# 64-bit weights read by a leaky rectifier on ScalarE that sets sign and exponent, no sign step on VectorE, and a new order of the work

## The chip, the core and the metric

The kernel runs on one core of a Trainium2 chip. The metric is the device time of one execution in microseconds (us), the median of three runs. The engines are called by the names of the profile: PE is TensorE (PEld its weight loads), DVE is VectorE, ACT is ScalarE, POOL is GpSimd, and SP issues the DMAs.

## The reference

Attention over a narrow window and over pooled blocks, and then a gated feed-forward network on its output, cut to what matters:

```python
# q, k, v: float32, B, H, S, D = 4, 8, 768, 64
k_sum = k.reshape(B, H, 24, 32, D).max(axis=3)
v_sum = v.reshape(B, H, 24, 32, D).mean(axis=3)
scores_l = where(abs(i - j) < 16, q @ k.T / 8, -1e9)
scores_s = q @ k_sum.T / 8 + log(32)
a = softmax(concat([scores_l, scores_s]))
attn = a @ concat([v, v_sum])                      # float32
x = attn.transpose(0, 2, 1, 3).reshape(3072, 512)
# w_gate, w_val: 512 x 1536, w_out: 1536 x 512, all float64
g = x @ w_gate
out = (g / (1 + exp(-g)) * (x @ w_val) @ w_out).astype(float32)
```

The three weight matrices come in 64 bits and go to the kernel as pairs of 32-bit words. The kernel makes a 32-bit float of each pair on the chip.

## The kernel before

**The products.** PE works on fp32r operands, which hold fewer bits than fp32. Every operand of the feed-forward products is therefore split into a high and a low part (`xh` and `xl` of attention's output, `hh` and `hl` of the hidden layer, two halves of one tile `w` or `o` for weights), and every product is made three times: high by high, high by low, low by high. Batch 0 goes through plain products: `g(j,h)` and `v(j,h)` for the twelve blocks j of 128 hidden columns and two halves h, and `D(0,...)` for the output. Batches 1 to 3 make seven products in the place of eight, with sums of weight blocks (`sumA..`), which are kept in DRAM (`sf`, `ss`, `wa`) and loaded again.

**Attention.** It goes in units (k,u), half a batch k and a pair of heads u, eight by four: scores (`SC`), `max`, `scl`, six `exp`, `eps`, `rcp` and `nrm` for the softmax, transposes of the probabilities (`PP0`, `PP1`, copied from PSUM by `pt0`, `pt1`), and the output (`XO`). `values` steps copy values and pooled values to the tiles `vw` and `vn`. Attention of the next batch runs between the feed-forward products of this one.

**The decode.** A weight block is decoded in five steps of 1024 columns, and there are 18 blocks (w0 to w11, and six of o). `abs` (L991, on ACT) writes the magnitude of the upper word, read as a 32-bit float, to the tile `m`. `clamp` (L995, DVE) holds it between two bounds. `shift` (L1001, DVE) moves its bits 3 to the left and masks them, by which eight bits of the 64-bit exponent come to the place of a 32-bit float's exponent. `sign` (L1008, DVE) takes the top bits of the raw word and sets them. `low` (L1014, DVE) adds three bits of the lower word. Then `hi` (ACT, the copy helper L513) rounds to fp32r, and `lo` (the subtraction helper L518, DVE or POOL) makes the rest. These blocks are decoded in the first 190 us, beside attention of batches 0 and 1 and the plain products of batch 0.

**The order.** Each step names the engines that may run it, its estimated cost, and the buffers that it reads and writes. `order()` is a list planner: at each turn the free engine takes the waiting step with the earliest due time. A table `NUDGES` shifts due times of single steps, gives a slack to some PE steps, and names the engine for some. `moved_behind()` then takes a hand-written table `MOVES` of 103 pairs: the first step of a pair is put right behind the second in its engine's row. The result is the order in which each engine issues its work. `WARM` names three PE steps ahead of which filler products run (5 ahead of SC(0,1), 6 ahead of XO(0,0), 1 ahead of PP1(0,2)).

Of the kernel before, what the change touches and what calls it, by code (L numbers as in the profile page):

```python
# [213 lines left out]
kt(0,1) -104.1; q(0,1) -74.3; vn(1) -74.9; kt(0,3) -72.8; q(0,2) +4.6; bias_sb +93.2; eps(0,1) -93.8 p; SC(0,3) s0.2  # L214
fv(3) -24.8 d; PP0(0,1) s0.6; pt0(0,1) +183.2 a; pt1(0,1) -26.3; FV(0) s4.6; fv(0) +54.5 d; nrm(0,2) +49 p
PP1(0,3) s0.6; XO(0,1) s1.3432; xh(1,0) +2.1 d; val2(3) +44.5 p; XO(0,3) s1.8; xh(3,0) +0.9 d; pt1(0,0) +44.3
raw_w0 -2.8; abs_w0 +68.8; lo_w0 -39.8; wa0 +27.3; odd1(0) +180.1; val2(0) -123.8 p; odd1(2) +53 a; val1(2) +4.8 p
val2(2) +1.3 p; abs_w1 +117.3; clamp_w1 +327.1; sign_w1 -90.9; q(1,0) +61.9; SC(1,0) s3.3; scl(1,0) -76.7 d
mul(0,0) -222.6; hh(0,0,0) -10.3 d; hl(0,0,0) +67.7 d; raw_w2 +31.8; sumA22_w2 +113.7 d; sumA12_w2 -32.4 d
scl(1,1) -72.2; exp0(1,1) +31.1; pt1(1,0) -84.2 d; values(1,1) +306.9; pt0(1,1) -39.1 d; pt1(1,1) -100.1  # L220
exp5(1,3) -130.7; eps(1,3) -102.1 p; raw_o0 +33.8; clamp_o0 +68.2; shift_o0 +158.4; low_o0 +72.2; raw_o2 +66.9
hi_o2 +67.7; raw_w3 -24.5; shift_w3 -150.5; sign_w3 +11.1; sumA11_w3 +76.8 d; values(1,2) +103.5 d; PP0(1,2) s1.9
PP1(1,2) s1.1; pt1(1,2) +145.2 d; values(1,3) +10.9 a; hl(0,1,1) -22.1 p; hh(0,2,1) -9.5 a; hh(0,3,1) -144.4 d
hl(0,3,1) +196.9 d; sf4 +110.8; hl(0,4,0) +78 d; kt(1,0) +154.6; pool(1,0) +198.5; vpool(1,0) +112.7; kw(2,1) +169.5
join(2,1) -183.7 a; exp4(2,0) +66; exp4(2,1) +59.7; eps(2,1) +55.4 p; lo_w5 +24.3 d; sumA22_w5 -122.2 p
silu(5,0) +105.9; hl(0,5,0) -46.5 p; PP0(2,0) s0.4; pt0(2,1) +21.4 d; values(2,1) +11.4 p; mul(5,1) +121.6
part(0,1,1) +60.9; part(0,1,2) +100.7; join(2,2) -267.6 p; join(2,3) -100.3 p; nrm(2,2) +43.9 d; SC(2,3) s1.5
nrm(2,3) -78.4 p; part(0,1,4) +34.9; abs_w6 +76.2; lo_w6 +123 p; hl(0,6,0) +84.9 d; pt0(2,3) +58.9 d; pt1(2,3) +63.6
# [5 lines left out]
shift_w9 +106.6; low_w9 -47; lo_w9 +182.3 p; wa9 -114.8; mul(9,1) -94.8; hh(0,9,1) +1.7 d; PP0(3,2) s5.3
values(3,3) +72.6 p; shift_w10 +191.5; lo_w10 +161.1 p; abs_o10 +60.5; clamp_o10 +204.2; shift_o10 +307.3
sumA22_w0 -33.5 p; sumA11_w0 -63.1 d; hi_w11 +92.3; sumA21_w1 -12.5 d; T3(1,0) +1.3 p; B11l(1,0) -69.3 p
B11h(1,1) -344.8; T3h(1,1) -126.8 d; T3l(1,1) +73.6 p; T4(1,1) -66.4 p; B22l(1,1) +42.9 p; q(4,0) -85.6
pool(2,0) +200.3; vpool(2,0) +53.6; exp2(4,0) +57.8; eps(4,0) -48.7 p; nrm(4,0) -2.8 p; ttr0(4,1) +110.7
exp1(4,1) +28.6; exp3(4,1) +86.5; eps(4,1) +82.4 p; s1(1,1) -125.4 d; hl(1,1,0) +90.2 p; mul(1,1,1) +79.4 d
hh(1,1,1) +97.8; ls(1,2) -73.1; c21(1,2) +190.8; pool(2,2) +155.6; vpool(2,2) +79.6; join(4,2) -39.6 p  # L240
join(4,3) +57.8 a; exp5(4,2) -52.6; exp0(4,3) +41.9; silu(1,3,0) +123.2; mul(1,4,1) +214.2; values(4,2) -142.4 p
join(5,0) +141.8 a; join(5,1) +167.7 a; eps(5,0) -13.1 p; SC(5,1) s5; ttr0(5,1) +131.9; eps(5,1) -4 p
nrm(5,1) -316.8 p; sumA22_w6 -24.1 p; s7(1,6) -21.7 a; hh(1,6,0) -272.9 d; hl(1,6,0) -15.2 p; mul(1,6,1) +1.6 p
PP0(5,0) s7.7; PP1(5,0) s2.8; values(5,1) -20.6 p; la(1,7) +104.2; ls(1,7) +86; sh(7) +115.8 a; sl(7) -19.1 p
ss(7) +117.1; mul(1,7,0) -26.2 p; hh(1,7,1) +55.6 d; sumA21_w8 -2.4 d; q(5,2) -28.4; XO(5,1) s4.6; exp4(5,2) +60.5
ttr0(5,3) -67.1; part(1,2,2) +80.9; sumA22_w9 +18.6 p; sumA12_w9 +55.6 p; sl(9) +14.2 p; values(5,3) +42.1 p
sumA12_w10 +28.4 p; sl(10) -26.9 p; sumA21_w11 +157 p; T3l(2,0) -80.7 d; T2l(2,0) +16.6 d; T1(2,1) +39.9 p
B11h(2,1) +120.8 d; join(6,1) -81.7 p; exp2(6,0) +67.3; exp3(6,0) +68; s1(2,1) -6.7 d; hh(2,1,1) +112.3 a
hh(2,2,1) -100.6 d; pt0(6,0) +0.6 a; pt1(6,0) +65.7 d; pool(3,2) +188.8; join(6,2) +56.6 a; join(6,3) +195.4 a
exp3(6,2) -70.8; exp4(6,2) -113; exp5(6,2) -27.7; eps(6,2) +37.4 p; exp1(6,3) -100.6; exp2(6,3) -28.7  # L250
exp5(6,3) +145; eps(6,3) +11.7 p; c22(2,3) -14.1 p; kw(7,0) -55.9; kw(7,1) -75.1; hl(2,8,1) +24.2 p
join(7,3) -10.1 p; vv(2,11) -98.1; u2(2,11) -100
# [41 lines left out]
)  # L294


def moved_behind(out):

    lists = {}
    for i, s in enumerate(out):  # L300
        s.rank = i
        lists.setdefault(s.engine, []).append(s)
    named = {s.name.replace(" ", "_"): s for s in out}
    for pair in MOVES.split("; "):
        x, y = (named[n] for n in pair.split())
        line = lists[x.engine]
        line.remove(x)
        line.insert(line.index(y) + 1, x)
    marks = set(lists.pop(None, []))
    done, again = set(), []  # L310
    while marks or any(lists.values()):
        heads = [l[0] for l in lists.values() if l] + list(marks)
        s = min((h for h in heads if all(o in done for o in h.after)), key=lambda h: h.rank)
        if s.engine is None:
            marks.remove(s)
        else:
            lists[s.engine].pop(0)
# [1259 lines left out]
```

## Time and profile before

| | us |
|---|---|
| median of three runs | 675.69 |
| the three runs | 677.05, 675.03, 675.69 |
| span of the profiled execution | 675.2 |
| PE busy | 661.9 (98%) |
| PE's weight loads busy | 609.4 (90%) |
| DVE busy | 502.0 (74%) |
| ACT busy | 374.1 (55%) |
| POOL busy | 129.8 (19%) |

The profile shows no other time of that execution than its span, which is 0.45 us under the median at two decimals (675.24). The granted clock of PE is at its upper level, 2.4 GHz, in all of the span. The page gives busy times over the whole span. The timeline of one engine says of every instruction how long the engine stood idle before it and which event ended that, and a table of windows gives busy times by stage.

### The profile page before, as it was taken

Reading aid. Unit: us, or ns where it says so; the run is one execution under the profiler, and the core shown is the slowest. Engines: PE = TensorE matmul, PEld = TensorE weight load, DVE = VectorE, ACT = ScalarE, POOL = GpSimd, SP = SyncE. Lnnn points to the kernel's source line nnn. Section 1 sums busy time; section 2 is a strip of 40 time slices with the busy share of each in tenths; the row PEclk is TensorE's granted clock in tenths of the full one; section 3 lists DMA queues with packets and bytes.
Section 4 is the critical chain, followed back from the end, with each engine's and each line's share of the span. In section 5 each row is a group of like instructions: output and inputs, shape, how many; then the busy total and the mean of one; then the engine's idle time right before and its main releaser. Section 6 shows DMA issues by size and latency. Waiting matters only on the chain.

```text
span 675.2 us, 13289 instructions
## 1 busy us (share of the span) xinstructions
PE 661.9 (98%) x5059; PEld 609.4 (90%) x5059; DVE 502.0 (74%) x1073; ACT 374.1 (55%) x901; POOL 129.8 (19%) x141
## 2 busy tenths in 40 slices
...
GB/s 343 387 296 289 310 227 332 263 248 337 310 238 160 247 312 217 318 274 218 241 205 250 160 295 154 225 215 111 252 67 201 155 253 76 230 97 222 106 109 95
DMA packets 39681, 152.71 MB, mean 226 GB/s; under 512 B 4352, under 2 KB 8896, under 8 KB 32704
## 3 DMA queue, kind: packets, MB, share of 16 engines
q1 hardware_dynamic: 39616, 151.85, 63.1%
...
## 4 chain that ended last, share of the span: by engine, by line
PE 74%; DVE 10%; DMA 3%; ACT 3%; issue 3%; POOL 0%; DVEq 0%; POOLq 0%; ACTq 0%
PE p L1197 36%; PE acc L1269 26%; PE xo L812 3%; PE g L1155 2%; PE pp L779 2%; DMA s<-ss 2%; PE v L1155 2%; PE sc L660 2%; DVE m_w L1008 1%; DMA s<-sf 1%; DVE m_w L1014 1%; DVE m_w L995 1%; DVE a L518 1%; DVE part L518 1%; ACT L1131 1%
## 5 line engine op out<-in xcount | busy, mean ns | idle before, releaser
L1269 PE MATMUL acc<-o,hh 128*128 128x512 f32 x570 | 177.8, 393 | 1.3 <-DVE a L518 1.3
L1269 PEld LDWEIGHTS acc<-o,hh 128*128 128x128 f32 x570 | 105.4, 188 | 23.9 <-DVE a L518 1.8
L1197 PE MATMUL p<-xh_T,s 128*128 128x384 f32 x432 | 122.7, 339 | 0.3 <-DMA s<-ss 0.2
L1269 PE MATMUL acc<-o,hl 128*128 128x512 f32 x285 | 111.4, 391 | 0.0
L1197 PE MATMUL p<-xh_B,wa 128*128 128x384 f32 x288 | 84.9, 335 | 0.0
L1197 PEld LDWEIGHTS p<-xh_T,s 128*128 128x128 f32 x432 | 79.0, 188 | 2.8 <-DMA s<-ss 1.3
L513 ACT CAST hh<-a 128x384 fp32r<-128x384 f32 x73 | 37.5, 513 | 71.9 <-DVE a L518 69.2
L1197 PE MATMUL p<-xl_T,s 128*128 128x384 f32 x216 | 72.3, 335 | 0.0
L513 ACT COPY s<-p 128x384 f32<-128x384 f32 x64 | 30.6, 478 | 73.4 <-PE p L1197 73.0
L518 DVE TENSOR_TENSOR part<-acc,part 128x512 f32<-128x512 f32 x71 | 47.4, 684 | 26.2 <-PE acc L1269 26.0
L1269 PEld LDWEIGHTS acc<-o,hl 128*128 128x128 f32 x285 | 53.5, 188 | 11.8 <-DVE hl L518 0.3
L518 DVE TENSOR_TENSOR hl<-a,hh 128x384 fp32r<-128x384 f32 x84 | 50.1, 597 | 14.9 <-ACT hh L513 12.1
L703 ACT ACTIVATE p<-p,nm 128x120 f32<-128x120 f32 x144 | 55.2, 385 | 4.4 <-DVE nm L691 4.0
L518 DVE TENSOR_TENSOR c<-p,u 128x384 f32<-128x384 f32 x72 | 39.6, 551 | 21.4 <-PE p L1197 21.3
L1155 PE MATMUL g<-xh_B,w 128*128 128x384 f32 x192 | 53.8, 339 | 1.7 <-ACT a L1131 1.3
L1155 PE MATMUL v<-xh_B,w 128*128 128x384 f32 x192 | 53.6, 338 | 0.0
L1197 PEld LDWEIGHTS p<-xh_B,wa 128*128 128x128 f32 x288 | 53.1, 188 | 0.1
L1197 PE MATMUL p<-xl_B,wa 128*128 128x384 f32 x144 | 48.2, 334 | 0.0
L1197 PE MATMUL p<-xh_B,s 128*128 128x384 f32 x144 | 42.6, 336 | 1.1 <-DVE v L518 1.1
L518 DVE TENSOR_TENSOR a<-c,a 128x384 f32<-128x384 f32 x65 | 36.9, 568 | 7.4 <-ACT a L1131 4.1
L1197 PE MATMUL p<-xh_T,wa 128*128 128x384 f32 x144 | 42.3, 334 | 0.0
L691 DVE CUSTOM_DVE_ANT_0 p<-sc,bias_sb 128x120 f32<-128x120 f32 x144 | 30.5, 276 | 14.4 <-PE sc L660 14.1
(161 smaller groups left out, 1360.6 us busy)
## 6 DMA issues: line engine op xcount, KB each, us to landing
...
```

Source lines behind the costliest of these rows:

```text
L513: nc.scalar.copy(out, in_)
L518: vector[e].tensor_tensor(out=out, in0=a, in1=b, op=op)
L660: nc.tensor.matmul(make(sc[h])[s * QT : (s + 1) * QT, c * KC + at : c * KC + at + x.shape[-1]], make(q)[hs, qs], x, start=not biased or c ...
L691: nc.vector.tensor_tensor_reduce(out=make(p)[:, i, :], in0=make(sc[g])[:, c * KC : (c + 1) * KC], in1=make(bias_sb)[:, 0 if n == 0 else 2 ...
L703: nc.scalar.activation(out=make(p)[:, i, :], in_=make(p)[:, i, :], func=AF.Exp, scale=-1.0, bias=make(nm)[:, i : i + 1], accum_out=make(sm ...
L779: nc.tensor.transpose(make(pp)[:KC, c * P : (c + 1) * P], make(p)[:, g * NT // 2 + c, :], make(id_sb))
L812: nc.tensor.matmul(ps[hs, qs], v, make(pt)[:, h, qs], start=True, stop=True)
L995: lambda e: nc.vector.tensor_scalar(out=make(m), in0=make(m), scalar1=F64_LO, scalar2=F64_HI, op0=ALU.max, op1=ALU.min), (), (m,),
L1008: lambda e: nc.vector.scalar_tensor_tensor(out=bits(), in0=high(), scalar=-0x40000000, in1=bits(), op0=ALU.bitwise_and, op1=ALU.bitwise_or ...
L1155: nc.tensor.matmul(t[:, :TOK], a, x, start=u == order_of[0] and i == 0, stop=u == order_of[-1] and i == 2,)
L1197: nc.tensor.matmul(t[:, :TOK], a, x, start=first and kk == 0 and n == 0, stop=kk == 1 and n == 2, skip_group_check=not first,)
L1269: nc.tensor.matmul(ps[:, :wide], a, w, start=j == js[0] and m == 0, stop=j == js[-1] and m == 2)
```

## The change

The decode loses a step, and its others change:

- `abs` becomes one ACT activation with the function Prelu: the upper word, read as a float, is scaled by 2^-112, and a negative result is multiplied by a slope of 2^32. That takes the exponent's bias off, and gives a negative weight an exponent that is 32 higher.
- `clamp` has new bounds, one of either sign. A magnitude over the top is held there.
- `shift` moves the bits 3 to the left and has no mask. The 32 in the exponent of a negative weight is one bit, which comes to lie where the sign is.
- `sign` is gone, on DVE 18 instructions. `low` stays as it was.

The table `NUDGES` is another one in all its entries, and `MOVES` with `moved_behind()` is gone. `WARM` is the same.

```diff
-F64_LO = float(np.uint32(0x38000000).view(np.float32))
-F64_HI = float(np.uint32(0x47EFFFFF).view(np.float32))
+REBIAS = 2.0**-112
+SIGNED = 2.0**32
+MOST = float(np.uint32(0x0FEFFFFF).view(np.float32))
+LEAST = -MOST * SIGNED
...
-SC(3,0) s0.8471; ttr1(3,0) +62; nrm(3,0) -34.1 p; ttr0(3,1) +95.2; mul(7,1) +143.9; clamp_w8 +56.1; clamp_o8 +118.8
...
+hh(0,0,0) +5.4; abs_w2 +154; lo_w2 +76.7; sumA12_w2 -125.1 d; sf2 +108.2; nrm(1,1) +55.1 p; hl(0,1,0) -49.1
...
-MOVES = (
-    "XO(0,0) PP1(0,0); SC(1,0) XO(0,2); v(0,0)b g(1,0); v(1,0) PP1(1,0); g(2,0) v(1,0); v(2,0) SC(1,2); g(3,0) v(2,0); "
...
-def moved_behind(out):
...
         plan.add(
-            f"abs {name}", {ACT: cost(ACT, "copy", n)},
-            lambda e: nc.scalar.activation(out=make(m), in_=high().bitcast(F32), func=AF.Abs), (raw,), (m,),
+            f"abs {name}", {ACT: cost(ACT, "copy", n) + 0.1},
+            lambda e: nc.scalar.activation(out=make(m), in_=high().bitcast(F32), func=AF.Prelu, scale=REBIAS, alpha=SIGNED),
+            (raw,), (m,),
         )
         plan.add(
             f"clamp {name}", {DVE: cost(DVE, "scalar", n)},
             lambda e: nc.vector.tensor_scalar(
-                out=make(m), in0=make(m), scalar1=F64_LO, scalar2=F64_HI, op0=ALU.max, op1=ALU.min
+                out=make(m), in0=make(m), scalar1=LEAST, scalar2=MOST, op0=ALU.max, op1=ALU.min
             ), (), (m,),
         )
         plan.add(
             f"shift {name}", {DVE: cost(DVE, "scalar", n)},
             lambda e: nc.vector.tensor_scalar(
-                out=bits(), in0=bits(), scalar1=3, scalar2=0x3FFFFFF8,
-                op0=ALU.logical_shift_left, op1=ALU.bitwise_and,
+                out=bits(), in0=bits(), scalar1=3, scalar2=None, op0=ALU.logical_shift_left,
             ), (), (m,),
-        )
-        plan.add(
-            f"sign {name}", {DVE: cost(DVE, "tt", n)},
-            lambda e: nc.vector.scalar_tensor_tensor(
-                out=bits(), in0=high(), scalar=-0x40000000, in1=bits(), op0=ALU.bitwise_and, op1=ALU.bitwise_or
-            ), (raw,), (m,),
         )
...
-    for s in moved_behind(order(plan.steps)):
+    for s in order(plan.steps):
```

Lines of the kernel after stand 56 lower than before in the attention and decode part (L991 is L935), and 62 lower in the feed-forward part (L1155 is L1093).

In the orders below, a name's last number is the tile's own, and numbers ahead of it are the unit or the block; `xN` counts like instructions in a row.

PE, at the end of the first attention units, before:

```order
L779 MATMUL pp0_0_0_478<-id_sb_99,p_0_0_352 120x128 x3
L779 MATMUL pp1_0_0_485<-id_sb_99,p_0_0_352 120x128 x3
L1310 MATMUL xo_0_0_520<-warm_81 128x128 x6
L812 MATMUL xo_0_0_520<-pt_0_0_494,vn0_232 64x64 x2
L812 MATMUL xo_0_0_520<-pt_0_0_494,vw_0_0_449 64x64 x2
```

PE at the same place, after:

```order
L723 MATMUL pp0_0_0_482<-id_sb_99,p_0_0_337 120x128 x3
L723 MATMUL pp1_0_0_489<-id_sb_99,p_0_0_337 120x128 x3
L723 MATMUL pp0_0_2_515<-id_sb_99,p_0_2_459 120x128 x3
L1248 MATMUL pp1_0_2_523<-warm_81 128x128
L723 MATMUL pp1_0_2_523<-id_sb_99,p_0_2_459 120x128 x3
L1093 MATMUL g_0_0_528<-xh_B11_0_1_475,w0_418 128x384
L1093 MATMUL g_0_0_528<-xl_B11_0_1_494,w0_418 128x384
```

The transposes of unit (0,2) and six of the twelve products of g(0,0) now come ahead of the six fillers and of XO(0,0), behind which they stood. Six of v(0,0)'s follow right behind XO(0,0), where before they came after the scores SC(1,0); the other halves still come after these.

ACT, where the rectifier (`silu`) of block 4's second half stands among the `exp` steps of batch 1, before:

```order
L703 ACTIVATE p_2_0_1471,sm_2_0_1482<-p_2_0_1471,nm_2_0_1472 128x120
L703 ACTIVATE p_2_1_1476,sm_2_1_1510<-p_2_1_1476,nm_2_1_1477 128x120
L1131 ACT_TABLE_LOAD
L1131 ACTIVATE a_0_4_1_1544<-g_4_1_1458 128x384
L703 ACT_TABLE_LOAD
L703 ACTIVATE p_2_1_1476,sm_2_1_1510<-p_2_1_1476,nm_2_1_1477 128x120
```

ACT at the same place, after:

```order
L647 ACTIVATE p_2_0_1461,sm_2_0_1485<-p_2_0_1461,nm_2_0_1462 128x120
L647 ACTIVATE p_2_1_1480,sm_2_1_1502<-p_2_1_1480,nm_2_1_1481 128x120
L1069 ACT_TABLE_LOAD
L1069 ACTIVATE a_0_4_1_1552<-g_4_1_1467 128x384
L935 ACTIVATE m_w6_1572<-raw_w6_1296 128x1024
L1069 ACTIVATE a_0_5_0_1591<-g_5_0_1530 128x384
```

All twelve `exp` of the two units now stand ahead of this `silu`, the pair of table loads around it is one load, and the Prelu of block w6 stands between two `silu` with no table load on either side. In the whole order ACT has 46 table loads before and 44 after.

POOL, from its last steps of unit (0,2) on, before:

```order
L758 TENSOR_TENSOR p_0_2_454<-p_0_2_454,ri_0_2_504 128x720
L752 TENSOR_SCALAR sm_1_1_729<-sm_1_1_729 128x6
L518 TENSOR_TENSOR hl_0_1_0_879<-a_0_1_0_803,hh_0_1_0_824 128x384
L515 COPY vw_1_1_766<-vs_0_305 24x768
L752 TENSOR_SCALAR sm_1_2_922<-sm_1_2_922 128x6
L518 TENSOR_TENSOR m_w2_556<-m_w2_556 128x256 x2
```

POOL at the same place, after:

```order
L459 COPY vw_1_1_562<-vs_0_289 24x768
L462 TENSOR_TENSOR w2_642<-m_w2_519,w2_642 128x1024
L459 COPY kw_2_0_582<-ks_1_0_735 128x6x24
L462 TENSOR_TENSOR m_w3_579<-m_w3_579 128x256
L702 TENSOR_TENSOR p_1_1_755<-p_1_1_755,ri_1_1_821 128x720
L462 TENSOR_TENSOR m_w3_579<-m_w3_579 128x256 x2
L459 COPY kw_2_1_600<-ks_1_1_940 128x6x24
L462 TENSOR_TENSOR hl_0_2_0_986<-a_0_2_0_899,hh_0_2_0_981 128x384
L462 TENSOR_TENSOR o2_984<-m_o2_891,o2_984 128x1024
L462 TENSOR_TENSOR o4_1168<-m_o4_1105,o4_1168 128x1024
```

The normalisation of unit (0,2) has gone from POOL to DVE, and the subtractions `lo` of w2, o2 and o4 have come from DVE to POOL. The fourth on POOL is now w7's; before, the four were those of w6, w7, w9 and w10.

## Rows read from the trace of the kernel before

**Rows 1.** The page: span; busy us, share of span, and instructions by engine.

```profile
span 675.2 us, 13289 instructions
PE 661.9 (98%) x5059; PEld 609.4 (90%) x5059; DVE 502.0 (74%) x1073; ACT 374.1 (55%) x901; POOL 129.8 (19%) x141
```

**Rows 2.** Windows, from and to in us; columns as the head line says.

```profile
core 0: us, PE busy (x) PEld busy (x) DVE busy (x) ACT busy (x) POOL busy (x), PEclk, DMA share, GB/s
40.00:60.00 20.00, 18.89 (x236) 17.54 (x235) 19.83 (x31) 18.98 (x45) 5.67 (x5) 1.00 0.88 314
...
125.00:150.00 25.00, 25.00 (x241) 23.14 (x239) 25.00 (x54) 20.14 (x49) 9.01 (x5) 1.00 0.78 277
...
500.00:600.00 100.00, 99.88 (x568) 92.50 (x567) 59.59 (x108) 37.07 (x77) 6.22 (x5) 1.00 0.51 182
```

**Rows 3.** PE's timeline: start, duration, instruction, [idle before it <- releaser].

```profile
19.64 0.42 PE L660 MATMUL sc<-kt,q 64*64 64x96 f32 x8 [0.55 <-ACT p L727]
...
27.86 0.27 PE L812 MATMUL xo<-pt,vn 120*64 120x64 f32 x1 [0.69 <-ACT pt L513]
...
42.51 0.84 PE L779 MATMUL pp<-id_sb,p 128*120 128x128 f32 x6 [0.75 <-DVE p L758]
...
52.95 0.44 PE L1155 MATMUL g<-xh_B,w 128*128 128x384 f32 x1 [0.36 <-DVE w L518]
...
109.11 0.44 PE L1155 MATMUL g<-xh_B,w 128*128 128x384 f32 x1 [1.33 <-ACT a L1131]
...
163.37 0.50 PE L1269 MATMUL acc<-o,hh 128*128 128x512 f32 x1 [1.34 <-DVE a L518]
...
235.73 0.44 PE L1197 MATMUL p<-xh_B,s 128*128 128x384 f32 x1 [1.11 <-DVE v L518]
```

**Rows 4.** Lines by shape: count | busy us, mean ns | idle before, releaser.

```profile
L513 ACT COPY s<-p 128x384 f32<-128x384 f32 x64 | 30.6, 478 | 73.4 <-PE p L1197 73.0
L1131 ACT ACTIVATE a<-p 128x384 f32<-128x384 f32 x36 | 17.7, 492 | 35.9 <-PE p L1197 35.9
L1008 DVE SCALAR_TENSOR_TENSOR m_w<-raw_w,m_w 128x1024 int32<-128x1024 int32 x12 | 14.8, 1237 | 0.1
L991 ACT ACTIVATE m_w<-raw_w 128x1024 f32<-128x1024 f32 x12 | 13.9, 1154 | 1.3 <-POOL w L518 0.7 <-DMA raw_w<-in_wgv 0.4
L518 DVE TENSOR_TENSOR w<-m_w,w 128x1024 fp32r<-128x1024 f32 x8 | 9.7, 1213 | 0.0
L1008 DVE SCALAR_TENSOR_TENSOR m_o<-raw_o,m_o 128x1024 int32<-128x1024 int32 x6 | 7.3, 1212 | 0.0
L758 DVE TENSOR_TENSOR p<-p,ri 128x720 f32<-128x720 f32 x21 | 22.2, 1067 | 0.3
```

**Rows 5.** Timeline of ACT ahead of PE's wait at 109 us.

```profile
107.28 1.28 ACT L1131 ACT_TABLE_LOAD   x1 [0.85 <-DVE hl L518]
...
108.57 0.49 ACT L1131 ACTIVATE a<-g 128x384 f32<-128x384 f32 x1
```

**Rows 6.** Timeline of the start: POOL and PE around unit (0,2).

```profile
25.41 1.50 PE L1310 MATMUL xo<-warm 128*128 128x128 f32 x12
...
26.75 1.39 POOL L758 TENSOR_TENSOR p<-p,ri 128x720 f32<-128x720 f32 x1 [0.95 <-DVE ri L755]
...
28.70 0.54 PE L779 MATMUL pp<-id_sb,p 128*120 128x128 f32 x3
...
33.14 0.42 PE L1155 MATMUL g<-xh_B,w 128*128 128x384 f32 x1
```

**Rows 7.** Timeline of DVE and POOL: a `clamp` alone, and one beside a `lo`.

```profile
143.58 0.67 DVE L995 TENSOR_SCALAR m_w<-m_w 128x1024 f32<-128x1024 f32 x1
...
151.96 2.39 POOL L518 TENSOR_TENSOR w<-m_w,w 128x1024 fp32r<-128x1024 f32 x1 [2.29 <-ACT w L513]
...
152.03 2.88 DVE L995 TENSOR_SCALAR m_w<-m_w 128x1024 f32<-128x1024 f32 x1
```

**Rows 8.** Timeline of DVE: the cast ahead of PE's wait at 236 us.

```profile
234.51 0.69 DVE L515 CAST s<-s 128x1024 fp32r<-128x1024 f32 x1 [2.27 <-DMA s<-sf]
```

More of the change, by code (lines that the diff above doesn't have):

```diff
@@ L213 @@
 NUDGES = """
[L214 to L228, printed above, removed]
@@ L229 @@
-values(2,3) -9.5 a; clamp_w7 +53.6; lo_w7 +40.1 p; hh(0,7,0) +28.8 d; hl(0,7,0) -43.5 p; kw(3,1) +26; XO(2,2) s3.7
-SC(3,0) s0.8471; ttr1(3,0) +62; nrm(3,0) -34.1 p; ttr0(3,1) +95.2; mul(7,1) +143.9; clamp_w8 +56.1; clamp_o8 +118.8
-sign_o8 +69.5; hi_o8 +60.5; mul(8,0) +126.3; pt0(3,0) +214 d; pt0(3,1) +39.3 d; pt1(3,1) +12.6 d
-values(3,0) -34.6 d; values(3,1) +53.1 d; part(0,2,1) -96.2; part(0,2,2) -82.4; kw(3,2) -66.4; XO(3,0) s0
-exp3(3,2) +78.1; exp4(3,2) -42.4; nrm(3,2) +116.8 p; exp2(3,3) +109.8; eps(3,3) -114.3 p; rcp(3,3) +37.4
@@ L234 @@
[L234 to L252, printed above, removed]
+vn(1) +2.9; q(0,2) +16; vn(0) +14.1; scl(0,1) -109.2 d; scl(0,3) +87.1 a; exp5(0,3) -17.7; nrm(0,3) +21.2 p
+fv(3) +3.2 d; scl(0,0) -0.7 a; exp1(0,0) +126.4; PP1(0,1) s1.13; pt1(0,1) +295.2 d; fv(0) -464.8 d; fv(1) +119.2 a
@@ new lines @@
+max0(0,2) -13.4; scl(0,2) -111.8 a; eps(0,2) +93.4 p; odd1(1) +2.9 a; xh(1,0) -234.9; val1(3) -32.9 p
+xh(3,0) +58.7 d; pt1(0,0) +60.6 a; abs_w0 -162.6; wa0 +143.9; odd2(0) +55.4 a; val2(0) p; odd2(2) -12.2 p
+val1(2) +66.1 p; val2(2) +67.5 d; XO(0,2) s1.094; wa1 +190.7; vw(1,0) +36.8; exp5(1,0) +9.4; nrm(1,0) +52.9 d
+hh(0,0,0) +5.4; abs_w2 +154; lo_w2 +76.7; sumA12_w2 -125.1 d; sf2 +108.2; nrm(1,1) +55.1 p; hl(0,1,0) -49.1
+pt0(1,0) +12.6 d; hh(0,2,0) +205.2 a; hl(0,2,0) -81.5 p; values(1,1) +4.1 p; scl(1,3) d; raw_o2 +63.6; lo_o2 +9.4 p
@@ new lines @@
+hi_w3 +2.8; hh(0,3,0) -12.6 d; values(1,2) +9.4 d; pt1(1,2) +10.4 d; part(0,0,0) +1.2 a; part(0,0,4) -158.1 d
+sumA11_w4 +122.4; lo_o4 -32.7 p; kt(1,0) -15.4; q(2,0) +113.5; kt(1,1) +93.2; vpool(1,1) -100.1; exp3(2,0) +3.6
+eps(2,0) d; exp3(2,1) +4; eps(2,1) +26.5 p; silu(4,1) +8.8; hh(0,4,1) +5.8 d; sumA22_w5 +30.5 p; silu(5,0) +59.1
+values(2,0) +269.2; pool(1,2) -35.7; vpool(1,2) -22; join(2,2) +80 a; join(2,3) -27 p; exp5(2,3) -101.7; hh(0,6,0) d
+pt1(2,2) -122.1 a; pt0(2,3) +34.8; clamp_w7 -241.3; q(3,0) +39.9; join(3,1) -136.4 a; SC(3,0) s1.451
@@ new lines @@
+exp4(3,0) +11.7; exp2(3,1) +108.1; exp4(3,1) +140.8; hl(0,7,1) +95.1 d; hh(0,8,1) a; part(0,2,2) +25.3; kw(3,2) +1.6
+join(3,2) +160.7 p; abs_w9 -35.4; clamp_w9 -162.3; hi_w9 -143.6; values(3,3) +8.3 p; raw_o10 +22; abs_w11 -35.1
+exp1(4,0) +166.7; exp3(4,0) +92.6; exp4(4,0) +39.1; eps(4,1) +273 d; silu(1,1,1) +62.4; mul(1,1,1) +67.1 p
+hl(1,1,1) -222.8 p; c21(1,2) -74.1; c22(1,2) -102.4 d; PP0(4,0) s0; q(4,2) +82.7; join(4,2) +75.3 d; SC(4,3) s7.979
+exp4(4,3) -122; s1(1,3) -2.8 d; s7(1,4) -123; mul(1,4,0) +461.6; pt1(4,2) a; pt0(4,3) +52 a; mul(1,5,1) +75.8
@@ new lines @@
+hh(1,5,1) -250.7 a; join(5,0) a; kw(5,1) +3; exp4(5,0) +66.2; hh(1,6,0) -63.2 a; pt0(5,0) -6.6 a
+values(5,1) -50.5 p; sumA22_w7 d; hh(1,7,0) +205.7 d; c22(1,7) +67.7 p; hh(1,8,0) -75.9 d; hl(1,8,0) -6.2 p
+c22(1,8) p; mul(1,8,1) -53.5 p; join(5,2) +261.3 a; kw(5,3) -14; join(5,3) -13.1 p; xf(5,0) -233 d; exp3(5,2) +26.3
+exp3(5,3) +38.1; sumA12_w9 -43.1; ss(9) -67; hl(1,9,0) +168.3 p; values(5,3) -33.1 a; sumA22_w10 +20 d; hh(1,10,1) d
+xf(5,3) +157.7 d; sumA22_w11 p; sumA21_w11 -74.5 p; s7(1,11) +125.1 a; mul(1,11,0) -15.4 p; mul(1,11,1) +58.4 d
```

29 lines of the change are left out of this document (6 added, 23 removed), and 17 rows, old and new, of the table MOVES.

## The prediction

> **What bounds the kernel now.** I read the page's first lines, then the windows by stage, then PE's timeline for the places where it stood idle and what ended each. PE is busy for 661.9 of 675.2 us, DVE for 74% and ACT for 55% [rows 1]. Over the whole span that says PE; stage by stage it says more. While weights are decoded, DVE has no spare time either: 19.83 of 20 us from 40 to 60, and 25.00 of 25 from 125 to 150, where PE is full as well [rows 2]. From 500 to 600 us, where nothing is decoded, DVE is busy for 59.59 of 100 us and PE for 99.88 [rows 2]. So removing work from DVE can help only in the first 190 us, and only by what PE waits there.
>
> PE's idle time is 13.3 us in all (675.2 less 661.9), and much of it is not for the taking: the head of the kernel, its tail, and first loads. The waits behind which a late engine stands are seven [rows 3]. At the start: 0.55 at 19.64 for an `exp`, 0.69 at 27.86 for a copy of probabilities, 0.75 at 42.51 for a normalisation on DVE, and 0.36 at 52.95 for a `lo`, together 2.35. In the decode stage: 1.33 at 109.11 for a `silu` on ACT, and 1.34 at 163.37 for a product of gate and value on DVE. Behind it: 1.11 at 235.73 for a `v` on DVE.
>
> **The sign step.** It leaves DVE's queue 12 times at 1237 ns and 6 times at 1212 [rows 4], 14.8 + 7.3 = 22.1 us. None of it is PE's own time, so its worth is what it takes off the waits above. Reading the orders up to the product a(0,4,0), the last of DVE's before the scores of batch 1, DVE has 20 two-operand decode steps before and 11 after, and 10 subtractions `lo` before and 8 after. That is 9 × 1.21 + 2 × 1.21 = 13.3 us less [rows 4]. Small steps that came from ACT and POOL to DVE (three of `hl`, a reduction, copies) take some of it back; I put them, less two normalisations that left, at 3.3. So DVE comes to that place some 10 us earlier in its own work, if nothing new holds it up.
>
> The wait at 109.11: ACT did not start the table load of that `silu` until 107.28, and the `silu` itself ran at 108.57 [rows 5]. PE waited for the buffer that it read. In the new order on ACT all twelve `exp` come ahead of it, where one was left behind it and needed a table load of its own. Those `exp` hang on the scores' `max` steps on DVE, which come 10 us earlier in DVE's work, and the wait is only 1.33. I take it as gone. The wait at 163.37 is DVE being late by its own queue, in a stage in which its queue was full [rows 2, 3]; with 10 us less ahead of it, and eight more signs still to go after a(0,4,0), I take this as gone too. What is late next is PE itself: from 125 to 150 us it has no idle time [rows 2].
>
> The wait at 235.73 stays. There DVE ran the cast of a weight sum that had arrived from DRAM only then, 2.27 idle and 0.69 of work [rows 8], and the new order has that cast, the load ahead of it and PE's products in the same sequence. Its price is 1.11 either way.
>
> **Prelu for Abs.** ACT's 18 activations of 1024 columns took 1154 ns with Abs [rows 4]. No Prelu is in the trace. The nearest pair of two functions on the same 384 columns is a copy at 478 ns and the rectifier at 492 [rows 4], 14 ns apart. The planner's figure in the change is 0.1 us more. So between 0 and 18 × 0.1 = 1.8 us of ACT's time; I take 0.02 each, 0.4 in all, by the nearer row. ACT is busy for 18.98 of 20 us from 40 to 60 [rows 2]; there some three fall, 0.06 at my value and 0.3 at the upper end. The table loads are 46 before and 44 after in the orders, none in front of a Prelu, so I charge none; the two fewer are 2 × 1.28 = 2.6 us of ACT's time [rows 5], the one at the `silu` of 109.11 among them, which is counted there.
>
> The Trainium skill, "ScalarE activation tables: per-element evaluation and per-set limits", section "What a function is on this engine", says that two functions in different sets are one table load apart, and that the same operands otherwise cost the same. The trace has the load at 1.28 us [rows 5]. If Prelu had a set of its own, 18 of the decodes would switch forth and back, by that rule an estimated 18 × 2 × 1.28 = 46 us of ACT, and the time would end far on the slow side. The order lists none there, so the sum stands without it.
>
> **The clamp and the shift.** They keep their size and operands; 0, with the noise of one run as the bound. Fewer operations in the shift may make it faster but hardly slower; it isn't PE's time.
>
> **The start.** Here the new order gives something up. Before, PE ran the six fillers of XO(0,0) from 25.41 on, XO(0,0) and then the transposes of unit (0,2) at 28.70; that unit's normalisation ran on POOL from 26.75 for 1.39 us, so it ended at 28.14 and PE did not wait for it [rows 6]. Now the transposes come first. PE is free for them from some 25.6 (it went on to the fillers at 25.41), and the normalisation is on DVE. A DVE normalisation takes 1.07 on average against POOL's 1.39, but the small step ahead of it goes to POOL, some 0.3; so the transposes can start at 26.75 + 0.3 + 1.07 = 28.1. PE then idles for 2.4 or 2.5 us [rows 4, 6]. Against it stand the 0.69 at 27.86 (XO(0,0)'s copy is done by then), and part of what else stood there; walking through the moved steps, the end of SC(1,0) comes to 36.1, against 33.14 before [rows 6], with 12 products done that took 2.08 before: 0.9 behind. From there on DVE is ahead (4 signs fewer before unit (1,0)'s normalisation), so that the 0.75 at 42.51 and the 0.36 at 52.95 should go, 1.11 back. I take the start as even at 60 us. Its bounds are −2.35 (all four waits gone, no new idle time) and +2.4 (the idle time is not won back).
>
> One load of 1 MB is moved ahead of another unit's operand on SP; the bytes are the same, so I charge 0, at most 0.5 for the scores that wait for it, inside these bounds.
>
> **The sum.** Span 675.24, less 1.33, less 1.34, start 0, Prelu 0 on the path: 672.57. The median stood 0.45 above the span: **673.0**, 0.4% under 675.69. About 0.3%, 2.0 us, is what the measurement can tell from no change.
>
> **Rivals.** *The start gains too* (all four waits of 2.35 gone, and no idle time ahead of the transposes): 673.0 − 2.35 = 670.7. For it: DVE and ACT have less to do there. Against: the transposes stand behind a softmax that isn't ready.
>
> *The start's loss is kept*: 1.5 to 2.4 us of idle time ahead of the transposes stay, and the decode stage gives 2.67 back: 674.5 to 675.4, no change. For it: from 53 us on PE waits little up to 109, so a loss of PE's own time is not made up anywhere.
>
> *POOL holds DVE up, slower.* Three `lo` of 1024 columns, w2, o2 and o4, now stand on POOL in the first 80 us, where DVE is full. Such a `lo` took POOL 2.39 us, and the `clamp` that DVE began beside it took 2.88 where another took 0.67 [rows 7]: 2.2 us of DVE for each one that meets a clamp or a shift. Three make 6.6, and with the start's 2.4 and a chain of attention that follows it, the relief of 10 us shrinks to 3 or less; the waits at 109 and 163 stay, and the start adds 2.4: 675.7 + 2.4 = 678. It decides from two of the three meetings on, if they fall ahead of unit (1,1)'s normalisation. Against it: four such `lo` stood on POOL before too, so these meetings need not be more than they were, only earlier.
>
> The Trainium skill, "SBUF — State Buffer", section "SBUF: two separate sides", gives the rule that speaks against this change: DVE and GpSimd share one pair of ports under an exclusive lock, held for a whole instruction, and the other one blocks fully. The trace agrees at that clamp [rows 7].
>
> *The change doesn't act*: the sign step was hidden, and the waits are set by something else: 675.7.
>
> **How the numbers follow.** My forecast, start even and the two waits gone, 0.43 (its spread of 1.5 us leaves 0.07 of that within 0.3%). The start gains too, 0.11. The loss is kept, 0.22. POOL holds DVE up, 0.22. No effect, 0.02. Faster by over 0.3%: 0.36 + 0.11 = 0.47. Within: 0.07 + 0.22 + 0.02 = 0.31. Slower: 0.22. The range goes from 670.5, just under the gaining case, to 678.5, just over the slow one; what is left out are start and POOL both at their worst, or more waits gone than I count. Cases of both signs hold most of the chance within it; the likeliest one's own range is 671.5 to 674.5.
>
> **What would show it.** Right: no row of PE over 0.3 us idle near 109 and 163; an idle time of some 2.4 us ahead of the transposes at 28, and none at 42 and 53; DVE under 95% from 125 to 150. The Prelu at 1.15 to 1.17 us with no table load in front. Wrong: clamps or shifts of over 2 us in the first 80 us beside POOL's `lo`, and PE's waits at normalisations or at `silu` larger than before; or the wait at 236 gone, which would mean that the reloads and not DVE set it.

## The result, and the profile after

The kernel after is slower: a median of 680.07 us (678.99 to 683.98, 6 runs) against 676.51 before (675.03 to 677.43, 6 runs), a ratio of 1.0062 with a 95% interval of 1.0039 to 1.0086. The forecast was 673.0 with a range up to 678.5. The profiled run took 679.47 us for a span of 677.8, so 1.7 us lie outside the span. One of the six executions of old_order below stood at the lower clock almost throughout (a mean granted clock of 0.557) and took 1087.34 us; it is left out of that kernel's median and ratio.

The first lines of the page after (they answer to [rows 1]):

```profile
span 677.8 us, 13260 instructions
...
PE 661.7 (98%) x5059; PEld 611.5 (90%) x5059; DVE 491.7 (73%) x1079; ACT 368.7 (54%) x898; POOL 110.6 (16%) x118
```

DVE works 10.3 us less, and PE is busy for as long as before; its idle time has grown from 13.3 to 16.1 us. PE's timeline says where (it answers to [rows 3]; start, duration, instruction, idle time before it and what ended it):

```profile
15.25 0.84 PE L723 MATMUL pp<-id_sb,p 128*120 128x128 f32 x6 [0.60 <-DVE p L702]
17.31 1.83 PE L781 MATMUL pv<-vn,mean_sb 128*24 128x128 f32 x28 [1.22 <-DMA vn<-in_vN]
20.51 0.45 PE L604 MATMUL sc<-kt,q 64*64 64x96 f32 x5 [1.37 <-DMA q<-in_qP]
24.88 0.27 PE L756 MATMUL xo<-pt,vn 120*64 120x64 f32 x1 [0.27 <-ACT pt L457]
29.94 0.86 PE L723 MATMUL pp<-id_sb,p 128*120 128x128 f32 x3 [3.34 <-DVE p L702]
40.75 0.42 PE L1093 MATMUL g<-xh_B,w 128*128 128x384 f32 x1
51.85 0.84 PE L723 MATMUL pp<-id_sb,p 128*120 128x128 f32 x6 [0.42 <-DVE p L702]
58.41 0.55 PE L723 MATMUL pp<-id_sb,p 128*120 128x128 f32 x3 [0.37 <-DVE xl_B L462]
66.62 0.98 PE L723 MATMUL pp<-id_sb,p 128*120 128x128 f32 x6 [0.61 <-DVE p L702]
114.28 0.44 PE L1093 MATMUL g<-xh_B,w 128*128 128x384 f32 x1 [0.81 <-ACT a L1069]
531.52 0.73 PE L1207 MATMUL acc<-o,hh 128*128 128x512 f32 x2 [1.44 <-DVE part L462]
```

Five waits up to 30 us sum to 6.80 us. The longest stands where the order fences showed the transposes of unit (0,2) ahead of XO(0,0). The waits at 163 and 236 us are gone, that at 109 has become 0.81 at 114, and there are new ones at 58, 67 and 531.

The waits are not all of it. In the windows behind the idle time (columns as in [rows 2]) the granted clock falls to one half, 1.2 GHz, while PE is full:

```profile
28.00:30.00 2.00, 0.06 (x1) 0.09 (x2) 1.97 (x4) 1.95 (x4) 1.04 (x2) 0.63 0.96 337
30.00:32.00 2.00, 2.00 (x10) 2.00 (x11) 1.94 (x3) 1.25 (x3) 0.00 (x0) 0.50 1.01 316
32.00:34.00 2.00, 2.00 (x8) 2.00 (x8) 1.45 (x3) 1.46 (x2) 0.00 (x0) 0.50 0.99 266
34.00:36.00 2.00, 2.00 (x16) 1.88 (x16) 0.18 (x1) 0.00 (x0) 0.00 (x0) 0.66 1.01 328
36.00:38.00 2.00, 2.00 (x32) 1.68 (x31) 0.66 (x2) 1.17 (x2) 0.00 (x0) 1.00 1.08 400
```

PE's first product behind the scores of unit (1,0) starts at 40.75, where it was 33.14 before [rows 6]. Twelve products of g(0,0) and v(0,0) (2.08 us in the prediction) are done by then that were not, so PE is 5.5 us late (7.61 less 2.08). At the end of the span only 2.6 are left: 2.9 us came back in between.

### The profile page after: what moved, and what is told of

The parts are those of the page before. It is cut to its first block, busy times and chain, and to the rows that moved or that the text cites. A ratio compares the mean times of both kernels' runs of the same rounds, so it can differ in the third digit from the quotient of the medians.

```text
span 677.8 us, 13260 instructions
## 1 busy us (share of the span) xinstructions
PE 661.7 (98%) x5059; PEld 611.5 (90%) x5059; DVE 491.7 (73%) x1079; ACT 368.7 (54%) x898; POOL 110.6 (16%) x118
## 4 chain that ended last, share of the span: by engine, by line
PE 86%; DVE 6%; DMA 5%; issue 1%; ACT 1%; SPq 1%; DVEq 0%
PE p L1135 37%; PE acc L1207 28%; PE v L1093 6%; PE g L1093 6%; PE xo L756 3%; PE pp L723 3%; PE sc L604 2%; DMA vn<-in_vN 2%; DMA vt<-in_vT 1%; DMA kw<-in_kW 1%; DMA kt<-in_kP 1%; DVE m_w L952 1%; DMA q<-in_qP 1%; DVE a L462 1%; SPq L476 1%
## 5 line engine op out<-in xcount | busy, mean ns | idle before, releaser
L1093 PE MATMUL g<-xh_B,w 128*128 128x384 f32 x192 | 54.7, 344 | 0.8 <-ACT a L1069 0.8
L1093 PE MATMUL v<-xh_B,w 128*128 128x384 f32 x192 | 53.6, 338 | 0.0
L462 DVE TENSOR_TENSOR v<-p,s 128x384 f32<-128x384 f32 x36 | 20.0, 556 | 28.8 <-PE p L1135 28.7
```

Of the source, the lines that this page charges most:

```text
L462: vector[e].tensor_tensor(out=out, in0=a, in1=b, op=op)
L1093: nc.tensor.matmul(t[:, :TOK], a, x, start=u == order_of[0] and i == 0, stop=u == order_of[-1] and i == 2,)
```

## Experiments

All ratios are against the kernel before, run beside it on the same chip. Names in the code are those of the kernel after, except in old_order, swap and the parts that follow the order of before.

**old_order and old_look: the new decode in the old order.** The order of before is kept on every engine by planning with the sign step's cost and issuing nothing for it:

```diff
         plan.add(
             f"sign {name}", {DVE: cost(DVE, "tt", n)},
-            lambda e: nc.vector.scalar_tensor_tensor(
-                out=bits(), in0=high(), scalar=-0x40000000, in1=bits(), op0=ALU.bitwise_and, op1=ALU.bitwise_or
-            ), (raw,), (m,),
+            lambda e: None, (raw,), (m,),
         )
```

Prelu, the bounds and the shift are those of the kernel after; NUDGES and MOVES those of before.

> The order of the kernel before on every engine, with the new decode: Prelu, the new bounds, the shift without a mask, and nothing at all in the place of the 18 sign steps. Theory (the start of the new order loses the time, and the decode itself wins some): no idle time over 0.8 us at 28 and the clock at its upper level, and the waits at 42, 53, 109 and 163 us (0.75, 0.36, 1.33, 1.34) shrink or go: 673 to 675, against 676.5 of before. Rival (the Prelu or the new bounds cost what the sign step gave): 676.5 or more, and Prelu rows of over 1.2 us.

> old_order once more, for its trace with an undisturbed clock. Theory: PE's waits at 109 and 163 us (1.33, 1.34) and two or more of those in the start are gone or halved, 4 us in all; Prelu at 1.15 us; no idle time over 0.8 us.

Measured: 0.9922 (0.9900 to 0.9945), a median of 672.00 us over five executions, a little under the theory's 673 to 675; old_look is the same kernel and took 671.87. Its page, and all of PE's waits after the first 10 us:

```profile
span 670.1 us, 13267 instructions
...
PE 659.9 (98%) x5059; PEld 609.7 (91%) x5059; DVE 482.9 (72%) x1055; ACT 373.4 (56%) x901; POOL 124.9 (19%) x141
```

```profile
14.83 0.22 PE L669 MATMUL sc<-parts_sb,id_r 128*128 128x120 f32 x1 [0.46 <-issue]
16.62 1.83 PE L839 MATMUL pv<-vn,mean_sb 128*24 128x128 f32 x28 [0.22 <-DMA vn<-in_vN]
19.90 0.42 PE L662 MATMUL sc<-kt,q 64*64 64x96 f32 x8 [1.06 <-ACT p L729]
23.74 0.65 PE L814 MATMUL xo<-pt,vn 120*64 120x64 f32 x3 [0.20 <-ACT pt L515]
28.11 0.27 PE L814 MATMUL xo<-pt,vn 120*64 120x64 f32 x1 [0.68 <-ACT pt L515]
30.61 0.27 PE L814 MATMUL xo<-pt,vn 120*64 120x64 f32 x1 [0.22 <-ACT pt L515]
52.80 0.44 PE L1155 MATMUL g<-xh_B,w 128*128 128x384 f32 x1 [0.93 <-DVE w L520]
645.75 0.44 PE L1197 MATMUL p<-xh_T,s 128*128 128x384 f32 x1 [0.40 <-DMA s<-ss]
```

The waits of [rows 3] at 42, 109, 163 and 236 us are gone, 0.75 + 1.33 + 1.34 + 1.11 = 4.53 us, and the span is 5.1 shorter. The two do not match one to one: other waits grew (0.93 at 52.80 for 0.36, 1.06 at 19.90 for 0.55), so that PE's idle time fell by 3.1 us, from 13.3 to 10.2; the other 2.0 are PE's busy time (661.9 to 659.9), spread over many lines, and why it fell is not shown. The Prelu costs what Abs did: the 12 of w take 1148 ns, against 1154 in [rows 4].

```profile
L993 ACT ACTIVATE m_w<-raw_w 128x1024 f32<-128x1024 f32 x12 | 13.8, 1148 | 2.0 <-DMA raw_w<-in_wgv 1.9
```

So the decode gains 0.78%, and the new order loses more than that. This kernel is faster than the kernel before and the kernel after.

**sign_back: the sign step's time in the new order.** Behind each shift DVE runs an operation of the sign step's size that changes nothing:

```diff
+                nc.vector.scalar_tensor_tensor(
+                    out=bits(), in0=high(), scalar=0, in1=bits(), op0=ALU.bitwise_and, op1=ALU.bitwise_or
+                ),
```

> The order of the kernel after on every engine, with a two-operand step on DVE behind each of the 18 shifts that changes nothing but takes the sign step's time. Theory: two of them stand ahead of the normalisation of unit (0,2), so the idle time of 3.3 us at 27 grows by up to 2.4, and the waits at 109 and 163 us come back: 684 to 687. Rival (the sign step was hidden beside PE's work): 680, as the kernel after.

Measured: 1.0263 (1.0240 to 1.0287), a median of 695.36, more than forecast. Not where the theory had it: the transposes of (0,2) wait 1.31 us, with 2.09 ahead of them at 28, together no more than the 3.34 of the kernel after. The softmax of unit (1,0) and the `silu` cost more:

```profile
28.00 0.37 PE L756 MATMUL xo<-pt,vn 120*64 120x64 f32 x1 [2.09 <-ACT pt L457]
...
56.47 1.51 PE L723 MATMUL pp<-id_sb,p 128*120 128x128 f32 x6 [3.69 <-DVE p L702]
...
124.92 0.69 PE L1098 MATMUL g<-xh_B,w 128*128 128x384 f32 x1 [4.59 <-ACT a L1074]
```

The sign step is not hidden in either order, and the new one has no room for it.

**start_new and start_old: half of one order and half of the other.** Both kernels plan twice, and take the steps of one order up to SC(1,1) and the remaining ones in the other order:

```diff
-    for s in order(plan.steps):
+    for s, s.engine in joined(plan.steps):
...
+    a, b = (old, new) if FIRST_PART == "old" else (new, old)
+    n = [s.name for s, _ in a].index(SEAM)
+    done = {s for s, _ in a[:n]}
+    return a[:n] + [x for x in b if x[0] not in done]
```

> The new decode without the sign step. Up to the scores SC(1,1) (about 41 us) every engine follows the order of the kernel after, behind it that of the kernel before. Theory: the idle time of 3.3 us at 27 and the fall of the clock behind it are there, and nothing behind 41 us makes them up: 679 to 681. Rival: 673 to 675.

Measured: 1.0007 (0.9993 to 1.0022), a median of 677.29, between the two cases. Its idle time ahead of the transposes of (0,2) is 3.34 again, and nothing over 0.6 us stands from there to 300 us. Against old_order it goes from 0.9922 to 1.0007, 0.85%, and most of that is the new start; 1.66 us of it (0.25%) is a wait at 304 us for a partial sum on DVE, which old_look does not have. The kernel after at 1.0062 has 0.55% more, by which the new order costs something behind the start too (0.3 to 0.8% by the two intervals).

> The new decode without the sign step. Up to the scores SC(1,1) (about 36 us) every engine follows the order of the kernel before, behind it that of the kernel after. Theory (the new order loses its time in the start): no fall of the clock and 672 to 674, as old_order at 672.4. Rival (the new order is worse behind the start too): 676 to 680, with PE's waits from 50 to 115 us as in the kernel after, or larger.

Measured: 1.0052 (1.0037 to 1.0066), a median of 680.09, which seems to contradict that. Its start is clean, but then PE stands still for the softmax of unit (1,0), and the clock falls behind that (0.50 from 52 to 54 us):

```profile
51.11 1.46 PE L841 MATMUL pp<-id_sb,p 128*120 128x128 f32 x6 [4.66 <-DVE p L820]
```

DVE's scaling step for it, 128x6 and 0.16 to 0.18 us elsewhere, took 2.36 while POOL ran the `lo` of w2, and a clamp ahead of it on DVE had waited for ACT's Prelu of w3:

```profile
39.65 0.70 DVE L1058 TENSOR_SCALAR m_w<-m_w 128x1024 f32<-128x1024 f32 x1 [1.76 <-ACT m_w L1053]
...
40.99 2.36 DVE L785 TENSOR_SCALAR nm<-nm 128x6 f32<-128x6 f32 x1
```

That Prelu was late by the seam. It writes the tile in which w1 was decoded; the old start ends w1's decode at 32.9 (`low` at 31.73, in the kernel after at 25.35), so the write of that tile to DRAM is issued late, and the new order has the Prelu of w3 ahead of the softmax. So this run doesn't price the new order behind the start.

**softmax_old.** In start_old, the softmax of unit (1,0) is moved ahead of silu(0,0) and of DVE's shift:

```diff
+SOFTMAX = "scl(1,0) max1(1,0); exp5(1,0) exp2(1,0); eps(1,0) exp5(1,0); silu(0,0) eps(1,0); scl(1,1) silu(0,0); rcp(1,0) max1(1,1); nrm(1,0) rcp(1,0)"
```

> start_old with the softmax of unit (1,0) moved ahead: on DVE its scl stands right behind its max steps and its normalisation behind those of unit (1,1); on ACT its last exp and eps stand ahead of silu(0,0). Nothing else is moved. Theory (start_old stood still for 4.66 us at 51 us since ACT's silu with two table loads came ahead of the exp of (1,0), a delay that the late start of the kernel after covers): the wait falls under 1.5 us, the clock stays up from 40 to 60 us, 674 to 676. Rival (POOL's lo of w2, which holds DVE's small steps for 2.4 us, or the whole of the new order from 36 us on): wait of 3 us or more, 678.5 to 680.

Measured: 1.0084 (1.0056 to 1.0111), a median of 683.03: neither. The wait at 51 did fall, to 1.30 at 49.83, but waits of 1.22 and 2.80 for the `silu` came, and the clock was at one half from 56 to 64 us. Its six executions part by the clock: three with a granted clock of 0.997 to 1.000 took 680.23 to 681.90 us, three with 0.992 and 0.993 took 684.15 to 684.89. The Prelu of w3 sat in front of it all. SP issued the write of w1's tile at 33.54, which landed after 6.2 us, and ACT stood still until then:

```profile
33.54 0.34 SPq L595 DMA_DIRECT2D whole<-m_w  x1
...
39.80 1.13 ACT L1054 ACTIVATE m_w<-raw_w 128x1024 f32<-128x1024 f32 x1 [4.35 <-issue]
```

This bears out the seam, and does not price the order behind it. It also shows POOL's hold once more: `low` of o0 took DVE 3.42 us beside POOL's `lo` of w2, against 1.21 for such a step.

**both: two moves in the start.** In the kernel after, XO(0,0) with its fillers goes back ahead of the transposes of (0,2), and a load is issued earlier:

```diff
+MOVES = "XO(0,0) PP1(0,0); raw_w1 q(0,2)"
...
-    for s in order(plan.steps):
+    for s in moved_behind(order(plan.steps)):
```

> The kernel after with two steps moved back in the start: XO(0,0) with its six fillers stands ahead of the transposes of unit (0,2) again, and the load of q for unit (0,2) is issued ahead of the raw weights w1. Theory: the wait of 1.37 us at 20.5 falls under 0.5, the idle time at 27 shrinks from 3.3 to some 1.5 since XO(0,0) needs copies that ACT ends at 29.6, and the clock stays at its upper level: 675.5 to 677.5. Rival (the loads set the start, and any idle time of over 1 us is enough for the clock to fall): 679 to 680.

Measured: 0.9999 (0.9987 to 1.0012), a median of 676.85, inside the theory's range. The scores' wait at 20.5 fell to 0.66 (the theory had under 0.5), and a wait of 1.54 stands at 24; the granted clock is at its upper level throughout the profiled run all the same, against the rival. XO(0,0) waits in two pieces in the place of the one idle time of 3.34:

```profile
29.23 0.33 PE L785 MATMUL xo<-pt,vn 120*64 120x64 f32 x2 [0.37 <-POOL vn L488]
30.61 0.27 PE L785 MATMUL xo<-pt,vn 120*64 120x64 f32 x1 [1.05 <-ACT pt L486]
...
37.37 0.42 PE L1122 MATMUL g<-xh_B,w 128*128 128x384 f32 x1
```

PE is 3.4 us earlier behind the scores of unit (1,0), at 37.37 for 40.75, and the span is 3.3 shorter (674.5 for 677.8), so what the two moves win in the start is kept to the end. The waits behind it stay: 0.70, 0.38, 0.34, 0.81 and 1.43 us at 49, 55, 63, 111 and 527, together 3.66, where the kernel after has 0.42, 0.37, 0.61, 0.81 and 1.44, together 3.65. So two moved steps win back the loss of 0.62% against the kernel before, and not the 0.78% that the decode alone gains. The load by itself does not do it (q_first, below); XO(0,0) by itself was not tried.

**fillers, q_first and fill_q: the clock apart from the wait.** Filler products shorten no wait; they only keep PE at work where it stood idle. The edits to the kernel after are the first line, the second, and both:

```diff
+WARM = {"SC(0,1)": 5, "PP0(0,2)": 13, "XO(0,0)": 6, "PP1(0,2)": 1}
...
+MOVES = "raw_w1 q(0,2)"
```

> The kernel after with 13 filler products more, ahead of the transposes of unit (0,2), where PE stood idle for 3.3 us; nothing else is changed. The normalisation that the transposes wait for comes no sooner, so this takes away the fall of the clock alone. Theory: the clock stays at its upper level from 26 to 36 us, and the work from 30 to 36 us takes 3.6 us instead of 5.9: 2.3 less, 677.5 to 678. Rival (the slow stretch is made up behind it, since PE then waits for others anyway): 679.5 to 680.

Measured: 1.0043 (1.0029 to 1.0057), a median of 680.1, near the rival's 679.5 to 680 and no gain that the intervals can tell. In the profiled run the clock fell too, but earlier, behind waits of 0.49 and 1.27 us at 15 and 17, and was back up at 28:

```profile
18.00:20.00 2.00, 1.84 (x17) 0.87 (x12) 1.40 (x5) 1.83 (x10) 1.91 (x2) 0.50 1.07 406
...
28.00:30.00 2.00, 2.00 (x23) 1.91 (x20) 1.51 (x5) 2.00 (x10) 0.57 (x2) 0.99 0.95 332
```

So the trace shows one fall in the place of another. But that doesn't account for the missing gain. Four of the twelve executions have a granted clock of 0.999 or 1.000 and took 679.39 to 680.60 us; the other eight, at 0.991 to 0.997, took 678.93 to 681.97. And in the trace PE is 0.74 us earlier behind SC(1,0) than in the kernel after (40.01 for 40.75), and has lost it at 52, where it waits 1.33 us for a normalisation in the place of 0.42. Ahead of that normalisation DVE's shift beside POOL's `lo` of w2 took 2.92 us:

```profile
39.78 2.92 DVE L946 TENSOR_SCALAR m_o<-m_o 128x1024 int32<-128x1024 int32 x1
```

The rows give the price of a fall in the stretch itself: from the transposes of (0,2) to XO(0,0), the same instructions take 35.12 − 31.75 = 3.37 us at 2.4 GHz here, and 35.86 − 29.94 = 5.92 in the kernel after, nearly all of it at 1.2. That is 2.5 us. In start_new, lo_dve and q_first the clock falls behind the same idle time (3.34, 3.34 and 3.32) for a shorter while, and the instructions take 4.81, 4.76 and 4.97.

```profile
31.75 0.49 PE L723 MATMUL pp<-id_sb,p 128*120 128x128 f32 x3
...
35.12 0.34 PE L756 MATMUL xo<-pt,vn 120*64 120x64 f32 x4
```

> The kernel after with one load moved: q of unit (0,2) is issued ahead of the raw weights w1. Theory: the wait of 1.37 us at 20.5 falls to 0.7 (the exp of ACT are next), but XO(0,0) stays behind the transposes of (0,2), so the idle time of 3.3 us and the fall of the clock stay: 679 to 680. Rival (the late load is the root of both): under 678, and a clock of 0.999 or more.

Measured: 1.0087 (1.0065 to 1.0108), a median of 682.33: neither case. The wait for q went, but the values' load is later (1.65 us at 17.7), and the clock fell twice, at 18 and at 32.

> q_first with 13 filler products ahead of the transposes of unit (0,2). The fillers shorten no wait for data; they only keep PE at work in the idle time of 3.3 us. Theory: with less idle time ahead of it than in the run with fillers alone, the clock stays at its upper level from 18 to 36 us, and this kernel is 1.3 to 2.3 faster than q_first. Rival (a fall of the clock costs nothing, since what PE does in it waits for others anyway): the same time as q_first.

Measured: 1.0060 (1.0041 to 1.0079), a median of 680.45, 1.9 us under q_first on the same chip. The intervals overlap a little, so the size is loose; the traces show one fall in the place of two. The fall at 18 stayed (0.50 from 18 to 20 us), against the theory; the one at 32 is gone. Ahead of the idle time both kernels are at the same product at the same time (26.08 and 26.09 us), and behind SC(1,0) fill_q is 0.98 us earlier (39.97 for 40.95): so much did the fall at 32 cost here. From 32 to 34 us, q_first and then fill_q:

```profile
32.00:34.00 2.00, 2.00 (x8) 2.00 (x7) 1.90 (x4) 1.81 (x3) 0.00 (x0) 0.50 1.00 234
```

```profile
32.00:34.00 2.00, 2.00 (x17) 2.00 (x16) 1.90 (x4) 1.68 (x3) 0.00 (x0) 1.00 1.02 302
```

**lo_dve: POOL's subtractions.** In the kernel after, the `lo` of w2, o2 and o4 go to DVE:

```diff
     for s in order(plan.steps):
+        if s.name in ("lo w2", "lo o2", "lo o4"):
+            s.engine = DVE
```

> The kernel after with the subtractions lo of w2, o2 and o4 on DVE, in the same place of the order, where they ran on POOL. Theory of the start: no gain, since these three stand behind the idle time at 27 us; DVE has 3.7 us more from 40 to 80 us, so 680 to 682. Rival (POOL's lo hold DVE's clamps and shifts up, one of 2.0 us at 42): the waits of PE at 52, 58 and 67 us (0.42, 0.37, 0.61) go, 678.5 to 679.

Measured: 1.0079 (1.0057 to 1.0101), a median of 682.82, a little over the theory's 680 to 682 and no faster than the kernel after. Behind waits of 0.34 and 1.09 us at 66 and 67 its clock fell a second time (0.50 from 68 to 70 us). POOL's hold on DVE is there, but taking it away by doing the work on DVE wins nothing.

**swap: one more exchange.** In old_order, `lo` of w3 goes ahead of `lo` of o0:

```diff
-    "lo_w3 lo_o0; rcp(1,1) max0(1,2); nrm(1,1) max1(1,2); xl(0,1) nrm(1,1); pt0(1,1) hh(0,2,0); sumA22_w2 pt0(1,1); "
+    "lo_w3 lo_o0; lo_o0 lo_w3; rcp(1,1) max0(1,2); nrm(1,1) max1(1,2); xl(0,1) nrm(1,1); pt0(1,1) hh(0,2,0); sumA22_w2 pt0(1,1); "
```

> old_order with one exchange on DVE: lo of w3 ahead of lo of o0. Theory: PE's last wait of that kernel in the decode stage, 0.93 us at 52.8 for lo of w3, falls under 0.3, and nothing is late next: 671.4 to 672, against 672.4 for old_order. Rival (it waits for ACT's cast of w3, which ends at 50.0, and the lo comes no sooner): 672.4.

Measured: 0.9947 (0.9927 to 0.9966), a median of 673.08, no better than old_order. The wait at 52.8 is gone, and a normalisation is late next:

```profile
54.73 1.07 PE L781 MATMUL pp<-id_sb,p 128*120 128x128 f32 x6 [1.08 <-DVE p L760]
```

## Why the prediction was wrong, point by point

- **The decode: the mechanism was right, the size low.** The sign steps were worth what they took off PE's waits, as the prediction said: 1.33 and 1.34 at 109 and 163 us, and 0.75 at 42. The prediction kept 1.11 at 236 as set by a reload. In old_look DVE waited 0.64 us for that reload, where it had been 2.27 [rows 8], and PE not at all; the whole came to 5.1 us of span. "Its price is 1.11 either way" was wrong.
- **The step that failed: the start taken as even.** Its bounds were −2.35 and +2.4; PE was 5.5 us late at SC(1,0). Three terms were mis-sized.
  - The load. One of 1 MB moved ahead of q(0,2) was charged 0, "at most 0.5". PE waited 1.37 for q at 20.51, where the scores before ran at 19.64 [rows 3], so they, and the `exp` behind them, came 0.87 later.
  - The idle time ahead of the transposes. 2.4 or 2.5 was forecast, 3.34 came, 0.9 more. The sum put the normalisation's start at 26.75 + 0.3. ACT's last `exp` began at 26.79, and after it came three engines in a row; the fence has the `exp` on ACT, `eps` on POOL, and on DVE a subtraction that stood in front, the reciprocal and the normalisation, at 1.27 and not 1.07:

```profile
26.79 0.40 ACT L671 ACTIVATE p<-sc,nm 128x120 f32<-128x120 f32 x1
...
27.45 0.24 POOL L696 TENSOR_SCALAR sm<-sm 128x6 f32<-128x6 f32 x1 [1.67 <-ACT p L671]
...
27.84 0.56 DVE L462 TENSOR_TENSOR xl_B<-xo,xh_B 128x384 fp32r<-128x384 f32 x1
28.31 0.18 DVE L699 RECIPROCAL ri<-sm 128x6 f32<-128x6 f32 x1
28.52 1.27 DVE L702 TENSOR_TENSOR p<-p,ri 128x720 f32<-128x720 f32 x1
```

  - The clock. It was in no term. The prediction moved six fillers behind the idle time and asked only what the wait would cost. The fillers had kept PE at work there; without them the clock fell, and the stretch behind took 2.5 us longer than at 2.4 GHz. How much of that reaches the end is open: fill_q, with one fall fewer, is 1.9 us faster than q_first, and fillers gained nothing.

  With the 0.9 us by which the prediction itself had PE behind at SC(1,0), the three (0.87, 0.9 and 2.5) come to 5.2 of the 5.5 us.
- **"The 0.75 at 42.51 and the 0.36 at 52.95 should go."** They went in old_order only in part (0.93 at 52.80 is left), and in the kernel after three others of 0.42, 0.37 and 0.61 came, although PE was 5 us late by then.
- **The wait at 109: "I take it as gone" had its reason upside down.** The prediction liked that all twelve `exp` stood ahead of the `silu`. But the trace of before has four `exp` behind the `silu`, not one, and so has old_look; the new order puts these four ahead of it, 4 × 0.38 us on ACT in a row, while PE waits for the `silu`. It is 0.81 in the kernel after and none in old_look. From the kernel after:

```profile
107.77 0.40 ACT L647 ACTIVATE p<-p,nm 128x120 f32<-128x120 f32 x1
...
111.95 0.38 ACT L647 ACTIVATE p<-p,nm 128x120 f32<-128x120 f32 x1
112.44 1.28 ACT L1069 ACT_TABLE_LOAD   x1
113.74 0.49 ACT L1069 ACTIVATE a<-g 128x384 f32<-128x384 f32 x1
```

- **The late stages.** The prediction had no term behind 236 us. A wait of 1.44 at 531 is new, for a partial sum on DVE.
- **The rivals.** The slow one named POOL's `lo` as the cause. The hold is real (2.36 where 0.16 to 0.18 is usual). The rule that the prediction cited from the Trainium skill ("SBUF — State Buffer", section "SBUF: two separate sides") agrees with that. But with these `lo` back on DVE (lo_dve) the kernel is no faster, so putting them on POOL isn't what made it slow. "The start's loss is kept" had the right place and a third of the size. Prelu at 0.02 us more and no table load in front was right.
- **The sum's base.** The prediction added 0.45 us to the span to reach the median. The runs show some 1.7 us outside the span (677.8 for 679.47), and 675.24 + 1.7 is 676.9, so the profiled execution of before was one of its slower ones. Over six executions before takes 676.51, so the base of 675.69 was 0.8 us low. That is on the side of the error, and a small part of the 7.1 us between 673.0 and 680.07.

In the ratios: the decode −0.78%, the new start +0.85% (0.25 of it the wait at 304 us in start_new), the new order behind the start +0.55%, together +0.62%. What the last part consists of was not tried apart; its rows are the waits at 52 to 67, 114 and 531 us, which stand in the run called both as well. In the start, the wait and the fall of the clock were not parted: the two moved steps took away both together.
